# Gate logits as four column-strip products and a sum, rank offsets in a 97th row, a bank held for values and logits

## The chip, the cores and the metric

One core of one Trainium2 chip. The metric is the device time of one execution in microseconds (us). The engines are TensorE (PE in the profile, its weight loads PEld), VectorE (DVE), ScalarE (ACT), GpSimd (POOL) and the sync engine (SP), which issues most DMAs. Each engine works through its own queue in order.

## The reference

```python
q_d, k_d, v_d = means over groups of 4 positions of q, k, v        # B,H,S,D = 4,8,576,64
out = repeat(softmax(scale*q_d@k_d.T) @ v_d, 4) \
    + softmax(where(|i-j|<4, scale*q@k.T, -1e9)) @ v
x = out.transpose(0,2,1,3).reshape(2304, 512)
logits = x @ w_gate + modality_bias[modality_id]                   # 512 x 8
e_idx = argmax(logits); gate_w = softmax(logits)[e_idx]
for e in range(8): x[mask_e] = gate_w * (relu(x[mask_e] @ w1[e]) @ w2[e])
h = x @ w_in; out = (max(h,0) + alpha*min(h,0)) @ w_out
```

## The kernel before

The kernel is one program of three parts: attention with the gate (`attention`, L16 to L373), the expert stage (`moe`, L612) and a dense second layer (`moe2`, L748). Attention goes over 4 batches with 6 tiles of 96 tokens each, 24 tiles in all. Each tile passes through small steps, and the loop at L356 traces them shifted against one another: `local1a`, `local1b`, `local1c` (scores in a band, softmax, its transpose into block-diagonal form), `local2` (values), `gate2` (transposes and logits), `gate3` (rank and row store). In turn n the loop traces `local1c` of tile n+1, `local2` of tile n, `local1a` of n+2, `gate3` of n-2, `gate2` of n-1 and `local1b` of n+2. Between them `go` (L360) traces pieces of the next batch's pooled attention (`stageA` to `stageP`) and, by `filler(4)`, four steps of the early expert.

The early expert (`Early`, L582): once some tiles are counted (turns in `EARLY`, L374), 128 rows of the likeliest expert are loaded and pushed through both of its layers, 640 matmul instructions at L596 for 5 slots of 128 rows, as filler between attention's matmuls. What is left is traced behind attention (L837, L839), and the expert stage's engines branch after the last of it (L874).

The order on each engine isn't the traced one. The tile framework plans it: every traced instruction has a priority (its place, moved ahead by `tc.high_priority`: 300 to 400 for the tile steps by `AHEAD`, L332), and the planner runs a model of the engines' times and gives each engine, whenever it is free in the model, the ready instruction of the best priority. On the chip each engine then takes its queue strictly in that order. The framework also puts in every semaphore wait.

PSUM has 8 banks: `pa` and `pb` for the early expert, and six here (L27): `sl` scores, `pv` values, `xb` transposed rows, `lg` logits, two `tp`. The rank tile `rk` and the counts share the bank of `lg` (L28, L821); each new tile of a bank waits until the last one is released.

The steps around the change:

- `local2` (L276): 8 value products into a `pv` tile of 128 x 4 x 96 (L283), each in one half of the array's columns. VectorE adds the pooled part (L286) and so makes `xt`, the tile's rows transposed: 128 partitions by 4 chunks of 96 tokens.
- `gate2` (L289): 4 transposes of `xt` (L294), which ScalarE copies to the row buffer (L295). Then the logits, 12 products: for each of 3 groups of 32 tokens, 4 chunks of 128 features are summed into 32 partitions of `p` (L299), with 32 columns of `xt` stationary and the 8 columns of the gate weights `wgs` moving. VectorE adds the bias (L300), finds the maximum and its index (L302, L303) and makes the one-hot `oh` (L305).
- `gate3` (L314): the rank of each token within its expert, summed in one bank: `tri` by `oh` (tokens before it in the tile), `ones` by `running` (tokens of the tiles before), and a single row of `ones` by `eoff`, the experts' row offsets 2304*e (L318 to L320). GpSimd makes the next `running` (L323), a rotating buffer of 96 x 8 (L126). VectorE picks out the rank (L325), and GpSimd stores the rows by an indirect DMA (L328).

An f32 product is two instructions in the profile (and two weight loads); a bf16 one and a transpose are one.

```python
for j in range(3):                                     # L297
    for c in range(4):
        nc.tensor.matmul(p[32*j:32*j+32],lhsT=xt[:,c,32*j:32*j+32],rhs=wgs[:,c],start=c==0,stop=c==3,tile_position=(0,32*j))
```

Of the kernel before, what the change touches and what calls it, by code (L numbers as in the profile page):

```python
# [4 lines left out]
F32=mybir.dt.float32; F32R=mybir.dt.float32r; BF16=mybir.dt.bfloat16; I32=mybir.dt.int32; U32=mybir.dt.uint32  # L5
# [4 lines left out]
N=B*S; DM=H*D; E=8  # L10
TT=96; NT=S//TT
# [4 lines left out]
def attention(ctx, tc, q, k, v, mod, wg, bias, xs, running, ps, eps, zeros, filler):  # L16

    nc=tc.nc
    sm=ctx.enter_context(tc.tile_pool(name="a_small",bufs=6))
    xp=ctx.enter_context(tc.tile_pool(name="a_rows",bufs=1))  # L20
    cp=ctx.enter_context(tc.tile_pool(name="a_const",bufs=1))
    X=[xp.tile([TT,4,132],F32,name=f"x{i}") for i in range(4)]
    wk=ctx.enter_context(tc.tile_pool(name="a_work",bufs=2))
    loading=ExitStack(); ld=loading.enter_context(tc.tile_pool(name="a_load",bufs=1))

    FIRST=dict(sd00="pa",sd01="pb",sd02="pa",sd03="pb")
    BANKS=dict(sl=1,pv=1,xb=1,lg=1,tp=2)  # L27
    SAME=dict(tl="tp",et="tp",pd="tp",sd="tp",rk="lg")  # L28
    def psum(shape,name):
        if name in FIRST: return eps.tile(shape,F32,tag=FIRST[name],name=name)  # L30
        k=name[:2]; k=SAME.get(k,k)
        return ps.tile(shape,F32,tag=k,name=name,bufs=BANKS[k])

    loads={}
    NB=S//128; TL=S-128*NB
    def load(b,which):
        if b>=B: return
        if which=="qk":
            for pair in (0,4,1,2,3):
                for n in "qk": load(b,(n,pair))  # L40
        elif type(which) is tuple:
            n,pair=which; src=(q if n=="q" else k)[b]
            if pair<4:
                t=loads[b,n,pair]=ld.tile([128,2,4*D],F32,tag="ld"+n,name=f"ld{n}{b}{pair}",bufs=3)
                nc.sync.dma_start(t,src[2*pair:2*pair+2,:512].rearrange("h (p r) d -> p h (r d)",r=4))
            else:
                t=loads[b,n,pair]=ld.tile([2*GT,4,4*D],F32,tag="lt"+n,name=f"lt{n}{b}")
                for h2 in range(2): nc.sync.dma_start(t[GT*h2:GT*h2+GT],src[h2::2,512:].rearrange("a (p r) d -> p a (r d)",r=4))
        elif which<2:
            w=loads["v",b,which]=ld.tile([128,4,4*D],F32,tag="ldv",name=f"ldv{b}{which}",bufs=2)  # L50
            nc.sync.dma_start(w,v[b,4*which:4*which+4,:512].rearrange("h (p r) d -> p h (r d)",r=4))
        else:
            w=loads["v",b,2]=ld.tile([128,4*D],F32,tag="ldw",name=f"ldw{b}")
            for h in range(H):
                nc.sync.dma_start(w[16*h:16*h+16],v[b,h,512:].rearrange("(p r) d -> p (r d)",r=4))
    load(0,"qk")
    wgs=cp.tile([128,4,E],F32,name="wgs")
    nc.sync.dma_start(wgs,wg.rearrange("(c p) e -> p c e",p=128))
    NTT=B*NT
    modi=cp.tile([TT,NTT,2],I32,name="modi")  # L60
    nc.sync.dma_start(modi,mod.rearrange("(t u) w -> u t w",u=TT))
# [44 lines left out]
    def iota_f(shape,pattern,base,cm,name,dt=F32):  # L106
        t=cp.tile(shape,dt,name=name)
        nc.gpsimd.iota(t,pattern=pattern,base=base,channel_multiplier=cm,allow_small_or_imprecise_dtypes=True)
        return t
    io8=cp.tile([TT,E],U32,name="io8"); nc.gpsimd.iota(io8,pattern=[[1,E]],base=0,channel_multiplier=0)  # L110
    eoff=cp.tile([1,E],BF16,name="eoff")
    eofff=iota_f([1,E],[[N,E]],0,0,"eofff"); nc.vector.tensor_copy(eoff,eofff)
    ones=cp.tile([TT,TT],BF16,name="ones"); nc.gpsimd.memset(ones,1.0)
    tri=cp.tile([TT,TT],BF16,name="tri"); nc.gpsimd.memset(tri,1.0)
    nc.gpsimd.affine_select(out=tri,in_=tri,pattern=[[1,TT]],compare_op=ALU.is_gt,fill=0.0,base=0,channel_multiplier=-1)
    tok=iota_f([TT,B*NT],[[TT,B*NT]],0,1,"tok")
# [3 lines left out]
    def bias_rows():  # L120
# [2 lines left out]
        for o,m,k2 in ((bsel,m0,0),(bse1,m1,1)):  # L123
            nc.vector.tensor_tensor(out=o,in0=m[:,:,None].to_broadcast([TT,NTT,E]),in1=bb[:,k2:k2+1].to_broadcast([TT,NTT,E]),op=ALU.mult)
        nc.vector.tensor_tensor(out=bsel,in0=bsel,in1=bse1,op=ALU.add)
    def new_running(n): return cp.tile([TT,E],BF16,tag="running",name=f"running{n}",bufs=3)  # L126
    running[0]=new_running(-1); nc.vector.memset(running[0],0.0)

    qd={}
    def stageA(b,pair,n):  # L130
# [145 lines left out]
    def local2(b,t):  # L276

        bd=st.pop((b,t)); w=V.pop((b,t))
        p=psum([128,4,TT],f"pv{b}{t}")
        for pair in range(4):  # L280
            for h2 in range(2):
                h=2*pair+h2
                nc.tensor.matmul(p[64*h2:64*h2+64,pair],lhsT=w[:,h],rhs=bd[:,h],start=True,stop=True,tile_position=(0,64*h2))  # L283
        xt=wk.tile([128,4,TT],F32,tag="xt",name=f"xts{b}{t}",bufs=3)
        c=t*TT//4
        nc.vector.tensor_tensor(out=xt.rearrange("p c (g r) -> p c g r",r=4),in0=p.rearrange("p c (g r) -> p c g r",r=4),  # L286
            in1=OT[b][:,:,c:c+TT//4,None].to_broadcast([128,4,TT//4,4]),op=ALU.add)
        st[b,t]=xt
    def gate2(b,t):  # L289

        xt=st.pop((b,t)); n=b*NT+t
        x=X[n%len(X)]
        px=psum([TT,4,128],f"xb{b}{t}")
        for c in range(4): nc.tensor.transpose(px[:,c],xt[:,c],ident)  # L294
        nc.scalar.copy(x[:,:,:128].rearrange("p a (c j) -> p c a j",c=4),px.rearrange("p c (a j) -> p c a j",a=4))  # L295
        p=psum([TT,E],f"lg{b}{t}")
        for j in range(3):  # L297
            for c in range(4):
                nc.tensor.matmul(p[32*j:32*j+32],lhsT=xt[:,c,32*j:32*j+32],rhs=wgs[:,c],start=c==0,stop=c==3,tile_position=(0,32*j))  # L299
        l=sm.tile([TT,E],F32,tag="l",name=f"l{b}{t}"); nc.vector.tensor_tensor(out=l,in0=p,in1=bsel[:,n],op=ALU.add)  # L300
        m8=sm.tile([TT,E],F32,tag="m8",name=f"m8{b}{t}"); i8=sm.tile([TT,E],U32,tag="i8",name=f"i8{b}{t}")
        nc.vector.max(out=m8,in_=l)  # L302
        nc.vector.max_index(out=i8,in_max=m8,in_values=l)  # L303
        oh=sm.tile([TT,E],BF16,tag="oh",name=f"oh{b}{t}")
        nc.vector.tensor_tensor(out=oh,in0=io8,in1=i8[:,0:1].to_broadcast([TT,E]),op=ALU.is_equal)  # L305
        ng=sm.tile([TT,4],F32,tag="ng",name=f"ng{b}{t}")
        gated[0]=d=nc.gpsimd.tensor_scalar(out=ng[:,0:1],in0=m8[:,0:1],scalar1=-1.0,scalar2=None,op0=ALU.mult)
        ex=sm.tile([TT,E],F32,tag="ex",name=f"ex{b}{t}")
        nc.scalar.activation(out=ex,in_=l,func=AF.Exp,bias=ng[:,0:1],scale=1.0,accum_out=ng[:,1:2])
        with tc.issue_after(d.ins): nc.gpsimd.tensor_copy(x[:,0,129:130],tok[:,n:n+1])  # L310
        gated[0]=d=nc.gpsimd.tensor_scalar(out=ng[:,1:2],in0=ng[:,1:2],scalar1=1e-9,scalar2=None,op0=ALU.add)
        nc.vector.reciprocal(out=x[:,:,128],in_=ng[:,1:2].to_broadcast([TT,4]))
        st[b,t]=(x,ng,oh)
    def gate3(b,t):  # L314

        x,ng,oh=st.pop((b,t))
        p=psum([TT,E],f"rk{b}{t}")
        nc.tensor.matmul(p,lhsT=tri,rhs=oh,start=True,stop=False)  # L318
        nc.tensor.matmul(p,lhsT=ones,rhs=running[0],start=False,stop=False)
        nc.tensor.matmul(p,lhsT=ones[0:1],rhs=eoff,start=False,stop=True)  # L320
        old=running[0]
        running[0]=new_running(b*NT+t)
        running[1]=nc.gpsimd.tensor_tensor(out=running[0],in0=old,in1=oh,op=ALU.add)  # L323
        jk=sm.tile([TT,E],F32,tag="jk",name=f"jk{b}{t}")
        nc.vector.tensor_tensor_reduce(out=jk,in0=p,in1=oh,scale=1.0,scalar=0.0,op0=ALU.mult,op1=ALU.add,accum_out=ng[:,3:4])  # L325
        ri=sm.tile([TT,1],U32,tag="ri",name=f"ri{b}{t}")
        nc.gpsimd.tensor_copy(ri,ng[:,3:4])
        d=nc.gpsimd.indirect_dma_start(out=xs[:],out_offset=bass.IndirectOffsetOnAxis(ap=ri[:,0:1],axis=0),in_=x.rearrange("p a d -> p (a d)"),in_offset=None,bounds_check=E*N-1,oob_is_err=False)  # L328
        tc.declare_no_dep(d.ins,group="early rows",reason="rows of other ranks than those of the early slots")
# [26 lines left out]
    for n in range(len(seq)+2):  # L356
        b,t=seq[n] if n<len(seq) else (B,0)
        if t==0 and b+1<B: fill=down(b+1)
        left=[P*(NT-t)-1]
        def go():  # L360
            step(max(1,left[0])); left[0]-=1
            filler(4)
        at(local1c,n+1)
        at(local2,n); go()
        go()
        go()
        at(local1a,n+2); go()
        at(gate3,n-2)
        at(loadV,n+3)
        at(gate2,n-1); go()  # L370
        at(local1b,n+2); go()
        yield n
# [538 lines left out]
```

## Time and profile before

| | us |
|---|---|
| median of 3 runs | 880.15 (875.56 to 884.18) |
| the profiled execution, its time | 872.86 |
| the profiled execution, its span | 871.1 |
| TensorE busy in the span | 813.2 |
| VectorE, ScalarE, GpSimd busy | 529.4, 361.4, 262.4 |

The profile is of one execution. Times in rows are microseconds from the start of the span; a row of a timeline gives the start, the time until its end, the engine, the line of the kernel, the operation and its output and inputs with their shape (for PE the stationary shape, then the moving one), how many instructions it merges, and in brackets how long the engine was idle before and what ended that. PE's rows overlap, since a matmul starts while the one before it is still leaving the array: what a group takes of TensorE is the time from its start to the start of the next group.

### The profile page before, as it was taken

To read this page: it belongs to the slowest core of one execution; us is meant where nothing else is said; L and a number is where in the kernel's file an instruction comes from. 1 tells how busy PE (TensorE), PEld (TensorE's weight loads), DVE (VectorE), ACT (ScalarE), POOL (GpSimd) and SP (SyncE) were. 2 spreads that over 40 slices of the span, in tenths; PEclk is the share of its full clock that TensorE was granted. 3 is DMA by queue.
4 is the path that set the end of the run, shared out by engine and by line. 5 is a ranking of instruction groups with operands and counts; after the bars stand their busy time and mean duration, and the time that the engine had idled before them with its cause. 6 is when DMAs were issued, how large, how long until landed. Compare 5 with 4: busy or idle time off the path is not lost.

```text
span 871.1 us, 16800 instructions
## 1 busy us (share of the span) xinstructions
PE 813.2 (93%) x6175; PEld 696.5 (80%) x6175; DVE 529.4 (61%) x1304; ACT 361.4 (41%) x863; POOL 262.4 (30%) x450
## 2 busy tenths in 40 slices
PE   5788899989997989899899999999999999999997
PEld 3466677778897989899898888888888888888895
DVE  6865866666444998989747997443444333433361
ACT  7687796885423655656442333111121111111120
POOL 9424645366332556534322342100010001000100
PEclk9786899999999999999999999999999999999999
DMA  7635666322333524549402342200020001000000
GB/s 190 174 98 157 189 176 171 103 59 55 78 86 91 99 86 110 111 135 245 107 25 75 132 147 71 85 1 0 11 82 1 0 1 64 3 0 1 38 13 25
DMA packets 96610, 71.74 MB, mean 82 GB/s; under 512 B 40457, under 2 KB 83977, under 8 KB 96521
## 3 DMA queue, kind: packets, MB, share of 16 engines
q1 hardware_dynamic: 93544, 61.02, 26.7%
q0 software_dynamic: 2976, 9.59, 3.2%
q8 instruction: 50, 0.82, 0.4%
q14 instruction: 40, 0.32, 0.2%
HBM read 76.43 MB, written 18.90 MB: 109 GB/s over the span
## 4 chain that ended last, share of the span: by engine, by line
PE 51%; issue 1%; DVE 1%; DMA 0%; POOL 0%; ACT 0%; POOLq 0%; DVEq 0%
PE oh L777 23%; PE oy L768 22%; PE y L721 3%; PE h L701 3%; DMA out<-o,ti 0%; POOL L L573 0%; DVE xwo L550 0%; DVE hl L704 0%; POOLq L907 0%; DVE w1l L542 0%; DVE xwi L549 0%; ACT o L793 0%; DVE xl L542 0%; ACT wih L541 0%; ACT yo L724 0%
## 5 line engine op out<-in xcount | busy, mean ns | idle before, releaser
L541 ACT CAST gh<-m 128x512 fp32r<-128x512 f32 (+1 forms) x80 | 44.5, 556 | 241.3 <-DVE m L780 239.4
L777 PE MATMUL oh<-oxh,wil 128*128 128x512 f32 (+1 forms) x320 | 118.9, 372 | 0.0
L777 PE MATMUL oh<-oxh,wih 128*128 128x512 f32 (+1 forms) x320 | 118.9, 371 | 0.0
L777 PE MATMUL oh<-oxl,wih 128*128 128x512 f32 (+1 forms) x320 | 118.6, 371 | 0.0
L779 DVE TENSOR_SCALAR m<-oh,al 128x512 f32<-128x512 f32 (+1 forms) x80 | 55.5, 694 | 91.1 <-PE oh L777 91.1
L794 POOL DMA_INDIRECT out<-o,ti x18 | 17.6, 979 | 307.8 <-ACT o L793 270.4
L768 PE MATMUL oy<-woh,gh 128*128 128x512 f32 x272 | 107.1, 394 | 0.0
L768 PE MATMUL oy<-wol,gh 128*128 128x512 f32 x272 | 106.7, 392 | 0.0
L768 PE MATMUL oy<-woh,gl 128*128 128x512 f32 x272 | 106.5, 393 | 0.0
L701 PE MATMUL h<-xh,w1h 128*128 128x256 f32 x224 | 66.5, 297 | 12.4 <-DVE hl L704 6.8
L542 DVE TENSOR_TENSOR gl<-m,gh 128x512 fp32r<-128x512 f32 (+1 forms) x80 | 48.9, 611 | 40.1 <-ACT gh L541 40.0
L777 PEld LDWEIGHTS oh<-oxh,wil 128*128 128x128 f32 x320 | 60.2, 188 | 11.8
L777 PEld LDWEIGHTS oh<-oxh,wih 128*128 128x128 f32 x320 | 60.1, 188 | 11.5
L777 PEld LDWEIGHTS oh<-oxl,wih 128*128 128x128 f32 x320 | 60.1, 188 | 11.3
L701 PE MATMUL h<-xl,w1h 128*128 128x256 f32 x224 | 65.2, 291 | 0.0
L701 PE MATMUL h<-xh,w1l 128*128 128x256 f32 x224 | 64.8, 290 | 0.0
L721 PE MATMUL y<-hh,w2h 128*128 128x256 f32 x224 | 62.1, 286 | 2.6 <-DVE yo L723 2.0
L721 PE MATMUL y<-hh,w2l 128*128 128x256 f32 x224 | 61.2, 287 | 0.9 <-DVE w2l L542 0.9
L768 PEld LDWEIGHTS oy<-woh,gl 128*128 128x128 f32 x272 | 51.1, 188 | 12.1
L768 PEld LDWEIGHTS oy<-wol,gh 128*128 128x128 f32 x272 | 51.0, 188 | 11.4
L721 PE MATMUL y<-hl,w2h 128*128 128x256 f32 x224 | 59.6, 286 | 0.5 <-DVE hl L704 0.4
L768 PEld LDWEIGHTS oy<-woh,gh 128*128 128x128 f32 x272 | 51.1, 188 | 11.0
(303 smaller groups left out, 1868.4 us busy)
## 6 DMA issues: line engine op xcount, KB each, us to landing
wraw<-in_moe_w SPq DMA_DIRECT2D x56, 512.0 KB
wi<-in_moe_w_in SPq DMA_DIRECT2D x32, 256.0 KB
wo<-in_moe_w_out SPq DMA_DIRECT2D x32, 256.0 KB
vw<-in_v SPq DMA_DIRECT2D x88, 64.0 KB
xs<-z SPq DMA_DIRECT2D x8, 528.0 KB
ldq<-in_q SPq DMA_DIRECT2D x16, 256.0 KB
ldk<-in_k SPq DMA_DIRECT2D x16, 256.0 KB
ldv<-in_v SPq DMA_DIRECT2D x8, 512.0 KB
```

Of the source, the lines that this page charges most:

```text
L541: nc.scalar.copy(hi,x)
L542: return lo_engine.tensor_tensor(out=lo,in0=x,in1=hi.bitcast(F32),op=ALU.subtract)
L701: nc.tensor.matmul(h,lhsT=a[:,c],rhs=b[:,c],start=n==0,stop=n==11); n+=1
L721: nc.tensor.matmul(y,lhsT=a[:,f],rhs=b,start=n==0,stop=n==23); n+=1
L768: nc.tensor.matmul(y[t],lhsT=a[:,ts],rhs=b[:,f],start=f==0 and k==0,stop=f==15 and k==2)
L777: nc.tensor.matmul(h[:,:n],lhsT=a[:,c,fs],rhs=b[:,c,:n],start=k==0,stop=k==11); k+=1
L779: nc.vector.tensor_scalar(out=m[:,:n],in0=h[:,:n],scalar1=0.0,scalar2=al[:,f:f+1],op0=ALU.min,op1=ALU.mult)
L794: nc.gpsimd.indirect_dma_start(out=out[:],out_offset=bass.IndirectOffsetOnAxis(ap=ti[:,t:t+1],axis=0),in_=o[:],in_offset=None,bounds_check ...
```

## The change

The gate weights are padded from 8 to 32 columns with zeros (a fill on GpSimd ahead of their load). The logits of a tile become 4 products, one for each chunk of 128 features, with the padded weights stationary and the tile's 96 tokens moving; chunk c lands in partitions 32c to 32c+31, side by side. VectorE copies the 128 x 96 result to SBUF (`lq`), and one product with a constant matrix `sume` (1 where the partition's number modulo 32 is the expert's) sums the four chunks and turns the result back to tokens by experts.

The three `running` buffers get a 97th partition that holds the experts' offsets, written once; `ones` gets a 97th row, and the offsets' own product goes.

The `pv` bank is held by one tile, `PV`, for the whole of attention: 384 columns for the values, the rest for the partial logits and their sum. The logits no longer use the `lg` bank, which the rank and the counts keep.

```diff
-    BANKS=dict(sl=1,pv=1,xb=1,lg=1,tp=2)
+    BANKS=dict(sl=1,xb=1,lg=1,tp=2)
...
+    PV=ps.tile([128,512],F32,tag="pv",name="pv")
...
-    wgs=cp.tile([128,4,E],F32,name="wgs")
-    nc.sync.dma_start(wgs,wg.rearrange("(c p) e -> p c e",p=128))
+    wgs=cp.tile([128,4,32],F32,name="wgs"); nc.gpsimd.memset(wgs,0.0)
+    nc.sync.dma_start(wgs[:,:,:E],wg.rearrange("(c p) e -> p c e",p=128))
...
-    eoff=cp.tile([1,E],BF16,name="eoff")
-    eofff=iota_f([1,E],[[N,E]],0,0,"eofff"); nc.vector.tensor_copy(eoff,eofff)
-    ones=cp.tile([TT,TT],BF16,name="ones"); nc.gpsimd.memset(ones,1.0)
+    eofff=iota_f([TT+1,E],[[N,E]],0,0,"eofff")
+    ones=cp.tile([TT+1,TT],BF16,name="ones"); nc.gpsimd.memset(ones,1.0)
+
+    sume=iota_f([128,E],[[-1,E]],128,1,"sume"); sumi=cp.tile([128,E],I32,name="sumi")
+    nc.vector.tensor_copy(sumi,sume)
+    nc.vector.tensor_scalar(out=sumi,in0=sumi,scalar1=31,scalar2=None,op0=ALU.bitwise_and)
+    nc.vector.tensor_copy(sume,sumi)
+    nc.vector.tensor_scalar(out=sume,in0=sume,scalar1=0.0,scalar2=None,op0=ALU.is_equal)
...
-    def new_running(n): return cp.tile([TT,E],BF16,tag="running",name=f"running{n}",bufs=3)
-    running[0]=new_running(-1); nc.vector.memset(running[0],0.0)
+    RUN=[cp.tile([TT+1,E],BF16,name=f"run{i}") for i in range(3)]
+    for t in RUN: nc.vector.tensor_copy(t[TT:TT+1],eofff[TT:TT+1])
+    running[0]=RUN[2][:TT]; nc.vector.memset(running[0],0.0)
...
-        p=psum([128,4,TT],f"pv{b}{t}")
+        p=PV[:,:4*TT].rearrange("p (c i) -> p c i",c=4)
...
-        p=psum([TT,E],f"lg{b}{t}")
-        for j in range(3):
-            for c in range(4):
-                nc.tensor.matmul(p[32*j:32*j+32],lhsT=xt[:,c,32*j:32*j+32],rhs=wgs[:,c],start=c==0,stop=c==3,tile_position=(0,32*j))
+        pq=PV[:,4*TT:]
+        for c in range(4): nc.tensor.matmul(pq[32*c:32*c+32,:TT],lhsT=wgs[:,c],rhs=xt[:,c],start=True,stop=True,tile_position=(0,32*c))
+        lq=wk.tile([128,TT],F32,tag="lq",name=f"lq{b}{t}")
+        nc.vector.tensor_copy(lq,pq[:,:TT])
+        p=pq[:TT,TT:TT+E]
+        nc.tensor.matmul(p,lhsT=lq,rhs=sume,start=True,stop=True)
...
-        nc.tensor.matmul(p,lhsT=ones,rhs=running[0],start=False,stop=False)
-        nc.tensor.matmul(p,lhsT=ones[0:1],rhs=eoff,start=False,stop=True)
+        n=b*NT+t
+        nc.tensor.matmul(p,lhsT=ones,rhs=RUN[(n+2)%3],start=False,stop=True)
         old=running[0]
-        running[0]=new_running(b*NT+t)
+        running[0]=RUN[n%3][:TT]
```

## Rows read from the trace of the kernel before

**Rows 1.** The page, its first lines: span, busy time, share and instructions.

```profile
span 871.1 us, 16800 instructions
```

**Rows 2.** Stretches: length, then busy time of PE, PEld, DVE, ACT, POOL; granted clock.

```profile
0.00:80.00 80.00, 58.55 (x583) 42.11 (x583) 52.76 (x151) 63.09 (x142) 41.17 (x116) 0.83 0.60 158
80.00:200.00 120.00, 106.45 (x1476) 87.36 (x1480) 80.57 (x324) 94.27 (x251) 63.85 (x144) 0.93 0.50 136
200.00:254.00 54.00, 54.00 (x757) 48.10 (x749) 25.50 (x138) 22.61 (x76) 25.97 (x67) 1.00 0.26 67
254.00:277.00 23.00, 22.83 (x201) 22.41 (x200) 14.76 (x63) 6.76 (x22) 5.91 (x7) 1.00 0.44 112
```

**Rows 3.** Timeline of PE, 274 to 283 us: the expert stage's first matmul.

```profile
282.24 0.58 PE L701 MATMUL h<-xh,w1h 128*128 128x256 f32 x1 [5.41 <-ACT w1h L541]
```

**Rows 4.** PE's waits, 0 to 255 us: total, times, longest.

```profile
PE sl L252 <- ACT kb L150: 11.0, 7, 3.2
...
PE et L215 <- DVE ed L197: 1.0, 2, 0.5
```

**Rows 5.** Timeline of PE, 242 to 256 us: logits, rank and early matmuls.

```profile
247.05 0.72 PE L299 MATMUL lg<-wgs,xts 128*32 128x8 f32 x24
247.70 2.05 PE L596 MATMUL ph<-Te,wraw 128*128 128x128 f32 x16
249.59 0.17 PE L318 MATMUL rk<-oh,tri 96*96 96x8 bf16 x1
...
249.74 0.20 PE L320 MATMUL rk<-eoff,ones 1*96 1x8 bf16 x1
249.87 1.16 PE L596 MATMUL ph<-Te,wraw 128*128 128x128 f32 x8
```

**Rows 6.** Timeline of PE, 140 to 180 us: shapes near to the new ones.

```profile
140.13 0.72 PE L205 MATMUL sd2t<-kdb,qdb 128*32 128x144 f32 x16
140.78 0.94 PE L596 MATMUL py<-eh,wraw 128*128 128x128 f32 x6
...
171.64 0.88 PE L283 MATMUL pv<-bd,vw 128*64 128x96 f32 x16
172.45 0.64 PE L294 MATMUL xb<-ident,xts 128*96 128x128 f32 x4
172.93 0.17 PE L318 MATMUL rk<-oh,tri 96*96 96x8 bf16 x1
```

**Rows 7.** Timeline of PE, 165 to 200 us: values and transposes in turn.

```profile
180.04 0.38 PE L283 MATMUL pv<-bd,vw 128*64 128x96 f32 x2
...
180.60 0.38 PE L283 MATMUL pv<-bd,vw 128*64 128x96 f32 x2
```

**Rows 8.** DVE's groups, 40 to 255 us: total and mean ns, then idle before.

```profile
L286 DVE TENSOR_TENSOR xts<-pv,ot 128x384 f32<-128x384 f32 x24 | 13.0, 543 | 4.7 <-PE pv L283 4.4 <-PE lg L299 0.2
...
L300 DVE TENSOR_TENSOR l<-lg,bsel 96x8 f32<-96x8 f32 x24 | 3.7, 154 | 14.4 <-PE lg L299 12.1 <-PE py L596 2.2
```

**Rows 9.** Timeline of all engines, 86 to 101 us: from VectorE to TensorE.

```profile
89.94 0.08 DVE L325 DVE_READ_ACCUMULATOR2_ANT ng<- 96x1 f32 x1
...
90.07 0.72 PE L299 MATMUL lg<-wgs,xts 128*32 128x8 f32 x24 [0.26 <-DVE ng L325]
```

**Rows 10.** Timeline of all engines, 224 to 256 us: values around the logits.

```profile
227.12 0.55 PE L283 MATMUL pv<-bd,vw 128*64 128x96 f32 x8
...
227.60 0.73 PE L299 MATMUL lg<-wgs,xts 128*32 128x8 f32 x24
...
228.25 0.38 PE L283 MATMUL pv<-bd,vw 128*64 128x96 f32 x2
228.36 0.16 DVE L300 TENSOR_TENSOR l<-lg,bsel 96x8 f32<-96x8 f32 x1 [2.82 <-PE lg L299]
```

**Rows 11.** Timeline of all engines, 0 to 24 us: the identity and its reader.

```profile
2.30 0.19 POOL masks.py:197 MEMSET ident<- 128x128 f32 x1
...
4.05 1.12 PE L140 MATMUL tpq<-ident,ldq 128*128 128x128 f32 x4 [4.05 <-POOL ident masks.py:199]
```

## The prediction

> **What bounds the kernel now.** I read the stage table first, then TensorE's waits, then its order of instructions around one gate step, then VectorE's groups. The profiled execution has a span of 871.1 us inside a time of 872.86 us [rows 1], 1.8 us around it, and it lies 7.3 us under the median of the three runs shown, 880.15 us. All sums below are differences, taken on the profiled execution and set on the median.
>
> The reader is to see four stages in the table [rows 2]. From 0 to 80 us TensorE is busy 58.6 of 80 us, at a mean granted clock of 0.83. From 80 to 200 us it is busy 106.5 of 120. From 200 to 254 us it is busy all 54.0 of 54, at clock 1.00: the last attention tiles, with the early expert's matmuls as filler between them. From 254 to 277 us it works off the rest of those early matmuls, 22.8 of 23 us. After that nothing of TensorE runs until 282.24 us, where the expert stage begins behind ScalarE's weight split [rows 3]. That gap begins when the last early output has left, so the end of the early work moves everything behind it. The change touches attention only; everything after 282 us I take as shifted, not altered.
>
> So the question is what happens to TensorE's queue up to 277 us. Up to 255 us its largest wait is for ScalarE's copies of the keys, 11.0 us in 7 times; the largest total that it waits for VectorE at one place is 1.0 us [rows 4]. In the first 200 us a shorter TensorE queue is partly given back to ScalarE; after 200 us it is gained in full, because there TensorE waits for nobody.
>
> **Part 1: the logits.** Before, a tile's logits are 12 products, 24 instructions (each f32 product is two). They start at 247.05 and the next matmul starts at 247.70: 0.65 us, 27 ns each [rows 5]. After, there are 4 products, 8 instructions, each on its own 32 columns of the array with 96 moving columns, and then one sum product, 2 instructions with 96 stationary and 8 moving columns. No row shows these shapes, so I bound them. The partial products: nearest is a group of the same array width with 144 moving columns, 16 in 0.65 us (140.13 to 140.78), 8 of them 0.33; by columns that is 0.22. At the old spacing of 27 ns, 8 take 0.22. The values' products, two column strips instead of four and the same 96 moving columns, take 0.81 for 16 (171.64 to 172.45), 0.41 for 8 [rows 6]. I take 0.30, between, nearest to the same array width. The sum: a transpose with 96 stationary columns takes 0.12 (four from 172.45 to 172.93 [rows 6]), so two instructions 0.24; at the low end 2 x 27 ns = 0.05, at the high end the 0.24 and one change of the array's layout, 0.17 [rows 7] (worked out below), 0.41. I take 0.26, by the row of its own width. So 0.56 against 0.65, 0.09 saved, between 0.38 saved and 0.17 lost. Over 24 tiles 2.2 us, from 9.1 saved to 4.1 lost.
>
> **Part 2: the rank.** Three bf16 products become two. The third starts at 249.74 and the next matmul at 249.87 [rows 5]: 0.13 us each, 3.1 us over 24 tiles. That is the high end; the low end is a third of what all three take (249.59 to 249.87), 0.09 us, 2.2 us in all. A product less in the queue has nothing to lose. One more row in the contraction of the remaining product I take at nothing: its instructions and their columns stay as they are.
>
> Together TensorE's queue is 5.3 us shorter, 0.22 us a tile. Eight tiles have their logits after 200 us, and gain in full: 1.8 us. For the other 16 I take half, since in the stages where they lie TensorE has waits that ScalarE ends: 1.8 us of 3.5. That is 3.6 us gained.
>
> **Part 3: the new copy.** VectorE gets one copy from PSUM a tile, 128 partitions by 96. Between the 8-column add, 0.154 us, and the 384-column add, 0.543 us [rows 8], the line gives 1.03 ns a column, so 0.245 us; 24 of them 5.9 us. After 200 us VectorE is busy 25.5 of 54 us and hides it. Before, it is busy about two thirds (52.8 of 80, 80.6 of 120) [rows 2], and TensorE hardly waits for it; but ScalarE and GpSimd wait for it too, so I charge a tenth, 0.6 us; from 0 to all of it, 5.9 us.
>
> **Part 4: the new wait.** The sum product stands in TensorE's in-order queue and waits for that copy. Everything behind it waits along: the transposes, the scores of tiles ahead and the early expert's matmuls. A release costs little: the accumulator read before the logits ends at 90.02 and their weights start loading at about 90.07 [rows 9], 0.05 us. With VectorE free, the wait is 0.05 for the hop, 0.245 for the copy and 0.05 back, 0.35 us, and 0.17 to 0.25 more for the last partial product to leave the array: 0.5 us in all. It is hidden whenever five early instructions (16 take 1.89 us, 247.70 to 249.59 [rows 5], 0.12 each) or a tile's scores stand between. From about 100 us on there is such filler at nearly every step, and the planner puts ready work ahead of a waiting instruction, so I take nothing. Without that cover it is 0.5 us a tile, 12 us in all, and more where VectorE has a queue.
>
> **Part 5: the held bank.** Values and logits now share one bank, and I take it that the framework keeps writer and reader of one bank apart: a tile's value products cannot run while VectorE reads another's logits. Before they did mix: the values' products at 227.12 and 228.25 stand around the logits at 227.60, and VectorE reads the logits at 228.36 [rows 10]. The bank's turn is 0.81 values, 0.54 add, 0.30 partial, 0.25 copy, 0.26 sum, 0.15 add and six hops of 0.05: 2.6 us, in a tile that takes about 240/24 = 10 us. I take nothing for it; the low end is a gain, since the logits no longer alternate with the rank product in one bank (the one wait for that in TensorE's list up to 255 us is the 0.26 us of [rows 9]), the high end the 2.6 us at the four last tiles, about 10 us.
>
> **Part 6: the start.** A fill of the padded gate weights stands ahead of the identity on GpSimd. TensorE's first transpose waits for the identity, 4.05 us [rows 11]. The identity's own fill, the same 128 x 128, is 0.19 us, so 0.2 us, and it goes straight through, as ScalarE copies without a pause after that. The gate weights' load now waits for the fill on the sync queue; twelve loads of queries and keys stand before it there, so nothing (a late fill would hold the value loads behind it: I allow 1 us). Six more tiny VectorE instructions, 0.15 us each by the 8-column add [rows 8], fall where VectorE waits for ScalarE anyway: 0 to 1 us, I take 0.
>
> **The sum.** 3.6 gained less 0.6 and 0.2: 2.8 us, so 870 us for the profiled execution and 877 us for the median.
>
> One rule is weighed here. The trace shows what alternating between array layouts costs: where two value instructions (51 ns each by [rows 6]) and one transpose (0.12) take turns, a round from 180.04 to 180.60 is 0.56 us instead of 0.22 [rows 7], 0.17 us a change. The Trainium skill, TensorEngine Tiling (Array Packing), section Key Properties, says that changing the tiling mode drains the engine. By that rule, which these rows bear out, the sum product costs nothing extra between full-width early matmuls and two changes among the scores; that is one of the rivals.
>
> **The rivals.** First, slower: the sum product stands right behind the partial products, or behind a VectorE queue, in most tiles. For it: VectorE is over 60% busy up to 200 us, and its queue holds adds and reductions of 0.4 to 0.7 us. Against it: filler, and the planner knows of the wait. Price 0.5 to 1.0 us a tile, 12 to 24 us, less the 5.3 saved: 7 to 19 us slower, 890 us in the middle. It decides from 0.22 us a tile on; from 0.6 us on it shows beyond 1%.
>
> Second, the changes of layout: in the 16 tiles before 200 us the sum falls among scores and values, two changes of 0.17 us each: 5.4 us, which takes the gain away: 880 to 883 us, no change.
>
> Third, faster by more: the separate banks let the gate run earlier, the early slots start sooner, and their matmuls fill TensorE's idle time of 13.5 us between 80 and 200 us [rows 2]. With half of that, 6.8 us on top of 2.8: 871 us. Against it: TensorE's waits there are ScalarE's, and the logits rarely waited for the bank.
>
> Fourth, the planner makes another order of the whole stage from its own durations; single orders can lie 5 us to either side. This widens the range, without a sign.
>
> **How the numbers follow.** The forecast (within 4 us of 877) has 0.42, the layout changes 0.15, the stall 0.23, the faster gate 0.20. A measurement of this kernel tells about 1%, 8.8 us, from no change. The faster gate is over that in most cases, the forecast and the planner's order in a few: 0.26 faster. The stall is beyond it in about four of five: 0.19 slower. That leaves 0.55. The range goes from 866 (faster gate, and logits at their low bound) to 889 (stall at the low half of its price).
>
> **What would show it.** Right: the 8 partial instructions in 0.22 to 0.41 us; the rank group 0.13 us shorter; about 0.25 us for the copy; the end of the early matmuls near 274 us instead of 277. Wrong: TensorE waits for the copy as a new row of over 3 us in its list of waits; full-width sums between scores; value products waiting for the logits' add; an end of the early work at or after 277 us.

## The result, and the profile after

| | before | after |
|---|---|---|
| median of the runs beside each other, us | 878.22 | 890.0 (886.02 to 891.08) |
| ratio, 95% interval | | 1.0132 (1.0089 to 1.0174) |
| span of the profiled execution, us | 871.1 | 888.4 |
| maximum of the last tile's logits on VectorE starts, us | 251.92 | 272.74 |
| last count on TensorE starts, us | 254.87 | 274.64 |
| first matmul of the expert stage starts, us | 282.24 | 297.29 |

Slower by 1.3%, 1 us outside the range of 866 to 889 us. In a later job, beside another set of runs of before, the same kernel stood at 1.0197 (1.0164 to 1.0231). The profiled execution of before is one of its faster ones (872.86 us, median 878.22), that of after lies at its median, so the spans differ by 17.3 us and the medians by 11.8. Of the 17.3 us, 15.1 are there when the expert stage starts. The page's first line, to [rows 1]:

```profile
span 888.4 us, 16132 instructions
```

The stages after, to [rows 2] (columns as there; the two behind the granted clock are the busy share of the DMA engines and the GB/s that they moved), with the stretch behind the early work:

```profile
0.00:80.00 80.00, 52.80 (x515) 38.14 (x517) 56.03 (x164) 63.82 (x144) 41.50 (x118) 0.86 0.59 149
80.00:200.00 120.00, 103.21 (x1291) 85.05 (x1290) 80.92 (x318) 90.65 (x247) 57.16 (x129) 0.92 0.51 131
200.00:254.00 54.00, 54.00 (x666) 47.85 (x657) 28.97 (x127) 23.02 (x74) 26.62 (x61) 1.00 0.40 82
254.00:277.00 23.00, 18.61 (x195) 16.90 (x193) 7.97 (x54) 5.51 (x21) 6.87 (x23) 0.98 0.16 40
277.00:297.00 20.00, 0.00 (x0) 0.00 (x0) 8.72 (x36) 1.43 (x2) 2.93 (x2) 0.50 0.34 81
```

TensorE is busy 156.0 us of the first 200, instead of 165.0, and 228.6 us of the first 277, instead of 241.8. What is new is the last line: 20 us in which it does nothing. Its timeline after, to [rows 3, 5, 6]:

```profile
95.41 0.45 PE L227 MATMUL et<-ident,edt 128*128 128x128 f32 x1 [3.17 <-DVE m L312]
...
240.71 0.17 PE L328 MATMUL rk<-oh,tri 96*96 96x8 bf16 x1
...
240.78 1.14 PE L606 MATMUL ph<-Te,wraw 128*128 128x128 f32 x8
241.85 0.37 PE L305 MATMUL pv<-xts,wgs 128*32 128x96 f32 x8
242.15 0.64 PE L302 MATMUL xb<-ident,xts 128*96 128x128 f32 x4
242.63 2.62 PE L606 MATMUL py<-eh,wraw 128*128 128x128 f32 x22
245.09 0.26 PE L309 MATMUL pv<-sume,lq 128*96 128x8 f32 x2
245.20 2.70 PE L606 MATMUL py<-eh,wraw 128*128 128x128 f32 x22
247.83 0.55 PE L291 MATMUL pv<-bd,vw 128*64 128x96 f32 x8
248.31 0.21 PE L328 MATMUL rk<-oh,tri 96*96 96x8 bf16 x1
248.38 0.19 PE L330 MATMUL rk<-run,ones 97*96 97x8 bf16 x1
248.49 0.55 PE L291 MATMUL pv<-bd,vw 128*64 128x96 f32 x8
...
269.16 2.25 PE L606 MATMUL py<-eh,wraw 128*128 128x128 f32 x18
...
274.64 0.17 PE L419 MATMUL cnt<-run,r_one 96*1 96x8 bf16 x1 [1.01 <-POOL run L333]
297.29 0.58 PE L711 MATMUL h<-xh,w1h 128*128 128x256 f32 x1 [22.48 <-DVE xwi L560]
```

And the same places before; the first four lines are for the part on the order:

```profile
66.93 1.55 PE L283 MATMUL pv<-bd,vw 128*64 128x96 f32 x16
68.41 0.49 PE L299 MATMUL lg<-wgs,xts 128*32 128x8 f32 x6
68.83 1.09 PE L294 MATMUL xb<-ident,xts 128*96 128x128 f32 x4
69.85 0.84 PE L299 MATMUL lg<-wgs,xts 128*32 128x8 f32 x18
...
254.87 0.17 PE L409 MATMUL cnt<-running,r_one 96*1 96x8 bf16 x1
254.96 7.41 PE L596 MATMUL py<-eh,wraw 128*128 128x128 f32 x64
262.21 7.47 PE L596 MATMUL ph<-Te,wraw 128*128 128x128 f32 x64
269.52 7.31 PE L596 MATMUL py<-eh,wraw 128*128 128x128 f32 x64
```

This is the finding. A count is a small product that adds up the tokens of each expert; the last one stands behind the last tile, and the plan of the expert stage is made of it. Before, the last count (L409) starts at 254.87 us with 192 early matmul instructions (96 products) behind it, 21.9 us of TensorE. After, the count is TensorE's last instruction ahead of the expert stage, at 274.64 us, and every early matmul is ahead of it. The early matmuls themselves end 5.4 us earlier than before (at 271.41 instead of 276.83 us), and TensorE's queue with the count ends 2.0 us earlier (at 274.81). But the expert stage needs what follows from the count: the plan, the first rows' load, their turn (transposition) and their split. Before, that ran under the early matmuls, which covered it; after, nothing of TensorE covers it. Its steps after, on the other engines:

```profile
275.18 0.18 DVE L459 TENSOR_REDUCE r_nr<-r_t 1x8 f32<-1x64 f32 x1
...
282.79 2.68 SPq L576 DMA_DIRECT2D L<-xs  x4
...
288.21 1.91 POOL L583 TENSOR_TENSOR L<-L 128x1024 f32<-128x1024 f32 x1 [10.09 <-DMA L<-xs]
290.16 1.25 DVE L585 STREAM_TRANSPOSE T<-L 128x1024 f32<-128x1024 f32 x1 [7.67 <-POOL L L583]
291.48 1.04 ACT L551 CAST xh<-T 128x1024 fp32r<-128x1024 f32 x1 [16.74 <-issue]
...
296.62 1.66 ACT L551 CAST w1h<-wraw 128x512 fp32r<-128x512 f32 x3 [4.09 <-DVEq L887]
```

Plan 7.6 us (275.18 to 282.79), load 5.4, turn and first half of the split of the rows 4.3 (to 292.52), then the branch, at which ScalarE waits 4.1 us, and the first weights' split, until 297.29.

Why is the count so late? One part shows in the middle of the timeline after. A tile's partial products start at 241.85, its sum only at 245.09, the next tile's values at 247.83: in both gaps stand 22 early matmuls, 2.5 and 2.6 us. The values must not enter the held bank before VectorE has read the sum, so one tile's turn is over before the next one's begins. TensorE hardly stalls for it. The group of its sum, up to 276 us (total us and mean ns, then idle before):

```profile
L309 PE MATMUL pv<-sume,lq 128*96 128x8 f32 x48 | 7.3, 224 | 0.4 <-DVE lq L307 0.4
```

VectorE's copy, in its groups from 40 to 275 us:

```profile
L307 DVE COPY lq<-pv 128x96 f32<-128x96 f32 x24 | 6.0, 249 | 12.9 <-PE pv L305 12.8
```

The idle time in front of all 48 sum instructions is 0.4 us. The wait is filled, but with the very matmuls that covered the plan.

The larger part is older than these turns. The sixth and the sixteenth maximum of the logits, before:

```profile
100.25 0.17 DVE L302 MAX8 m<-l 96x8 f32<-96x8 f32 x1
...
199.82 0.17 DVE L302 MAX8 m<-l 96x8 f32<-96x8 f32 x1
```

And after:

```profile
111.39 0.15 DVE L312 MAX8 m<-l 96x8 f32<-96x8 f32 x1
...
215.14 0.17 DVE L312 MAX8 m<-l 96x8 f32<-96x8 f32 x1
```

The gates are 11.1 us late at the sixth of 24 tiles, 15.3 at the sixteenth and 20.8 at the last. The pause at 92 to 95 us (last section) lies just ahead of the sixth; what else delayed them before 215 us was not taken apart.

### The profile page after: what moved, and what is told of

It reads as the page before. It is cut to its first block, busy times and chain, and to the rows that moved or that the text cites. A ratio compares the mean times of both kernels' runs of the same rounds, so it can differ in the third digit from the quotient of the medians.

```text
span 888.4 us, 16132 instructions
## 1 busy us (share of the span) xinstructions
PE 800.9 (90%) x5815; PEld 686.1 (77%) x5815; DVE 546.3 (61%) x1334; ACT 361.0 (41%) x863; POOL 265.7 (30%) x452
## 4 chain that ended last, share of the span: by engine, by line
PE 52%; DVE 6%; DMA 4%; issue 3%; SPq 1%; POOLq 0%; ACT 0%; DVEq 0%; ACTq 0%
PE oh L787 23%; PE oy L778 22%; PE h L711 4%; PE y L731 3%; DMA wi<-in_moe_w_in 2%; DMA L<-xs 2%; DVE w2l L552 1%; DVE xwi L561 1%; DVE xwi L560 1%; DVE hl L714 1%; DVE xwi L559 1%; DVE w1l L552 1%; DMA wo<-in_moe_w_out 0%; DMA out<-o,ti 0%; DVE xl L552 0%
## 5 line engine op out<-in xcount | busy, mean ns | idle before, releaser
L711 PEld LDWEIGHTS h<-xh,w1h 128*128 128x128 f32 x224 | 45.4, 203 | 34.0 <-ACT w1h L551 23.3
L787 PEld LDWEIGHTS oh<-oxh,wil 128*128 128x128 f32 x320 | 60.2, 188 | 11.8
```

The source lines that it names most:

```text
L711: nc.tensor.matmul(h,lhsT=a[:,c],rhs=b[:,c],start=n==0,stop=n==11); n+=1
L787: nc.tensor.matmul(h[:,:n],lhsT=a[:,c,fs],rhs=b[:,c,:n],start=k==0,stop=k==11); k+=1
```

## The experiments

The products behind the last count are early products of the planned order (of 320 in all, two instructions each); the two times are starts in each kernel's trace, as above. The ratio is to runs of before in the same job.

| kernel | products behind the last count | last count, us | first expert matmul, us | ratio |
|---|---|---|---|---|
| before | 96 | 254.87 | 282.24 | 1 |
| after | 0 | 274.64 | 297.29 | 1.013, 1.020 |
| rank alone | 104 | 267.58 | 301.23 | 1.021 |
| bank alone | 80 | 262.37 | 289.62 | 1.012 |
| partials and sum alone | 0 | 289.11 | 310.43 | 1.038 |
| rank, partials and sum | 0 | 283.87 | 304.84 | 1.033 |
| rank and bank | 64 | 268.05 | 291.85 | 1.011 |
| after, 64 products held back | 64 | 265.54 | 291.64 | 1.012 |
| after, 88 held back | 88 | 267.40 | 296.33 | 1.014 |
| before, plan uncovered | 0 | 279.96 | 298.01 | 1.014 |
| before with one tiny copy | 83 | 277.94 | 305.10 | 1.028 |
| before with the setup alone | 80 | 260.72 | 287.85 | 1.002 |
| after, sum in the rank tiles' bank | 44 | 264.00 | 283.77 | 1.010 |
| after, another order | 0 | 274.32 | 296.55 | 1.017 |
| sum in the rank bank, order 2 | 100 | 259.58 | 289.42 | 1.011 |
| sum in the rank bank, order 3 | 83 | 261.04 | 288.72 | 1.003 |
| before, another order | 96 | 263.71 | 291.78 | 1.000 |

The times come from one profile each and rank the kernels only roughly: from the first expert matmul to the end of the span the profiles take 587 to 596 us. The setup alone starts the expert stage 5.6 us later than before and is no slower; the sum in the rank tiles' bank starts it 1.5 us later and is 1.0% slower.

**The price of the lost cover.** In the kernel before, the last count was queued behind the last early matmul, nothing else changed (the first cut of the edit, which keeps hold of that matmul as `early.last`, is left out):

```diff
...
-            with tc.high_priority(500): router.plan(psum,running,cp)
-        early.go(len(early.steps)-10)
-        mark=early.mark
-        early.finish()
+            early.go(len(early.steps)-10)
+            mark=early.mark
+            early.finish()
+            with tc.high_priority(500), tc.issue_after(early.last.ins): router.plan(psum,running,cp)
```

> The kernel before, nothing of the change in it; only the plan's count is queued behind the last early matmul on TensorE, so that all 320 early products stand ahead of it instead of 224. Cover theory: TensorE's work ends at about 277 us as before, the count with it, TensorE then idles 22 us as in the changed kernel instead of 5.4, the expert stage starts at 296 to 301 us and the time is 885 to 893 us beside some 876. If the plan were hidden anyway, or the loss lay in the logits' own chain, the time stays within 5 us of the kernel before.

1.0135 (1.0064 to 1.0206). Its timeline of TensorE:

```profile
279.96 0.17 PE L409 MATMUL cnt<-running,r_one 96*1 96x8 bf16 x1
298.01 0.58 PE L701 MATMUL h<-xh,w1h 128*128 128x256 f32 x1 [17.88 <-ACT w1h L541]
```

That is a loss of the changed kernel's size, 15.8 us at the start of the expert stage against 15.1 and nearly the same ratio, without any part of the change. (3.2 us of the 15.8 are early matmuls that end at 280.0 instead of 276.8, in a slightly other order.) So an uncovered plan is enough for a loss of this size.

**Giving cover back.** The changed kernel with early steps held until the last count is traced: 64 products (its edit is shown, cut), then 88.

```diff
     def go(self, n):
+        if self.hold: return
...
-        early.go(len(early.steps)-10)
+        early.hold=False
+        with tc.issue_after(router.marks[ENG.PE].ins):
+            early.go(len(early.steps)-10)
...
```

> The changed kernel, with the last early slot's matmuls held back until the last count has been issued on TensorE (traced behind attention and queued behind the count). If what costs the time is that the early matmuls ran ahead of the last gate steps and left the plan and the first row load uncovered, the count comes 10 us or more earlier than 274.6, some 15 us of early matmuls lie behind it, the expert stage starts 10 to 20 us before 297 us, and the time is 870 to 880 us. If the tiles are late by the length of their own chains, with or without filler between them, the count stays after 265 us and the time near 885 to 890, or above, since the held matmuls then come on top.

> The changed kernel with 88 of the 320 early products queued behind the last count, in place of none (the first trial held 64). Cover theory: the count comes at 258 to 264 us, early matmuls run until about 282, the expert stage starts some 5 us after them, 870 to 880 us. Rival: without filler in the last tiles TensorE idles there by as much as is won behind, and the time stays at 882 to 888 us as in the first trial.

64 held: 1.0123 (1.007 to 1.0176), the expert stage 5.7 us earlier than after; 88 held: 1.0142 (1.007 to 1.0213), 1.0 us earlier. Neither gained time that can be told from the changed kernel's, and both missed what the cover alone had promised, 870 to 880 us. With 64 held the count came at 265.54 us, 9.1 earlier than after but 10.7 later than before. With 88 it came no earlier, and the last early matmuls left at 291.1 us, 5.2 us before the expert stage: now the early work itself was late.

The trace with 64 held shows two reasons. Attention's own chain is late already where filler still stands: the twentieth maximum starts at 244.77 us, before at 228.56. And without filler the new waits lie open and the granted clock falls. Two rows of TensorE's timeline, and a stretch (columns as in [rows 2]):

```profile
251.78 0.34 PE L309 MATMUL pv<-sume,lq 128*96 128x8 f32 x2 [0.38 <-DVE lq L307]
252.38 0.88 PE L291 MATMUL pv<-bd,vw 128*64 128x96 f32 x16 [0.26 <-DVE l L310]
```

```profile
257.00:266.00 9.00, 4.10 (x32) 2.82 (x32) 3.31 (x23) 1.37 (x5) 4.20 (x14) 0.50 0.16 44
```

TensorE is busy 4.1 of 9 us at a granted clock of 0.50, and the first 64 early matmul instructions behind the count take 9.4 us (265.64 to 275.06), before 7.3 (254.96 to 262.21). So these two runs do not measure the cover alone.

**One part, or two.** The rank part alone, the bank alone, the partial products and sum alone (in the bank of `lg`), and two pairs; each is the corresponding lines of the diff.

> The kernel before with the rank part alone: three running buffers with a 97th row, one product less per tile. Bank theory and round-trip theory: the gate's last count stays near 255 us with some 20 us of early matmuls behind it, and the 24 x 0.13 us make the time 1 to 3 us shorter, 875 to 878 us beside 878. Order theory (any edit makes the planner lay the stage out anew): the last count can move by 5 us or more, and the time by as much, either way.

> The kernel before with the held bank alone: the 12 old logit products write behind the values in one tile that is held for all of attention. Bank theory: the value products of a tile wait for the logits' add of an earlier one, the last count moves from 255 us to 265 us or later behind the early matmuls, TensorE idles over 15 us before the expert stage, 885 to 892 us. Round-trip theory: no copy and no second product here, so 876 to 880 us with the last count near 255.

> The kernel before with the four partial products, the copy and the sum alone; they lie in the old bank of the logits, which they share with the rank, and the values rotate as before. Round-trip theory: the planner lays early matmuls between partial products and sum in each tile, the last count moves to 265 us or later, 885 to 892 us. Bank theory: the last count stays within 5 us of 255, 874 to 880 us.

> The changed kernel without the held bank: rank and the four partial products with their sum, these in the old bank shared with the rank. Round-trip theory: the count comes last on TensorE, with no early products behind it and 20 us or more of idle time, 887 to 906 us. Bank theory: the cover is back, 96 products or so lie behind the count, 872 to 880 us.

> The changed kernel without the partial products and their sum: rank and held bank with the 12 old logit products. Round-trip theory: some 60 to 100 early products lie behind the count, TensorE's idle time before the expert stage is 5 to 9 us, 876 to 886 us. Bank theory: the count comes late behind the early products, with 15 us or more of idle time, 886 to 895 us.

All were slower: 1.0212 (1.0162 to 1.0262), 1.0115 (1.0063 to 1.0166), 1.0378 (1.0327 to 1.043), 1.0326 (1.0255 to 1.0397) and 1.011 (1.0037 to 1.0183). Of these, the two with the sum have their count last, the three without it keep 64 to 104 products behind. The sum alone was slower than either theory had it (905.8 us against 885 to 892 at most), and the bank alone fell between them. But the rank alone, which takes a product away and adds only three small copies to the setup, lost 2.1%, more than the whole change. Its work doesn't explain that, and it led to the next two.

**The order by itself.** The kernel before with one copy of 8 numbers more in its setup; and with the setup of the change (the fill of the padded weights, the constant matrix, three copies into the 97th partition), its loop as before.

```diff
+    nul=cp.tile([1,E],BF16,name="nul"); nc.vector.tensor_copy(nul,eofff)
     running[0]=new_running(-1); nc.vector.memset(running[0],0.0)
```

> The kernel before with one copy of 1 x 8 elements more on VectorE in the setup, and nothing else: no work to speak of (0.2 to 1.5 us of VectorE near 20 us). But the planned order is another one: 237 early products instead of 224 stand ahead of the last count, and TensorE's queue has 88 changes of the array's layout ahead of the first count instead of 69. If the order is what costs (the rank alone had 95 such changes and lost 2%): slower by 0.5 to 2%, 882 to 893 us beside 877, the gates late by the end of the first batch. If only the work counts: no change, within 0.3%.

> The kernel before with the setup of the change and nothing of its loop: the fill of the padded weights, the constant matrix, the three copies into the 97th partition (the loop doesn't read them). If the start is what delays the gates (first maximum at 61.2 us instead of 55.5): slower by 2 to 6 us, with the first maximum at 59 to 62 us and that lag kept to the last count. If the start is absorbed, as the two traces suggest at the second and third tile: within 0.3%, unless the order differs again; planned are 240 early products ahead of the count and 51 layout changes ahead of the first count, fewer than before.

The one copy cost 25 us: 1.0283 (1.0241 to 1.0324), more than the 0.5 to 2% expected. The whole setup cost nothing that can be told: 1.0018 (0.9982 to 1.0055). So a planned order alone can be worth more than the change. One thing that the copy's order does, in its timeline of TensorE:

```profile
63.96 0.45 PE L295 MATMUL xb<-ident,xts 128*96 128x128 f32 x1
64.34 0.59 PE L284 MATMUL pv<-bd,vw 128*64 128x96 f32 x4
64.86 0.45 PE L295 MATMUL xb<-ident,xts 128*96 128x128 f32 x1
```

A stretch of it, in the table of stretches (columns as in [rows 2]):

```profile
64.00:72.00 8.00, 8.00 (x64) 4.86 (x63) 3.46 (x14) 4.08 (x8) 3.35 (x8) 0.50 0.42 110
```

And the same stretch before:

```profile
64.00:72.00 8.00, 6.49 (x60) 4.58 (x62) 4.00 (x13) 6.81 (x16) 1.35 (x2) 0.59 0.52 132
```

Transposes and values of two tiles take turns one by one, at a granted clock of 0.50: 3.90 us for 16 values and 4 transposes (63.96 to 67.86, where the next group starts). Before, at a like clock, they stand apart, 1.48 and 1.02 us. The Trainium skill, TensorEngine Tiling (Array Packing), section Key Properties, says that a change of the tiling mode drains the engine; the trace agrees so far as the turns cost time, 1.4 us more a tile at the low clock. The kernel with the rank alone shows the same turns between 62 and 76 us. How much of the 25 us they make was not taken apart.

**Is it order or structure?** The planner's priorities were moved by small amounts, and the orders it made were counted: in all 20 of the changed kernel the 320 early products are ahead of the last count, in 20 of before 224 to 268. These are planned orders, and no trace shows them, but one of the changed kernel was run:

```diff
-    AHEAD={local1a:300,local1b:400,local1c:300,loadV:350,local2:300,gate2:300,gate3:350}
+    AHEAD={local1a:300,local1b:415,local1c:300,loadV:365,local2:360,gate2:300,gate3:350}
...
-            with tc.high_priority(250): f[0](*f[1:])
+            with tc.high_priority(290): f[0](*f[1:])
```

> The changed kernel with other priorities of the planner (values 360 instead of 300, their loads 365, scores 415, pooled steps 290): the same instructions in another order, 219 changes of layout up to the last count instead of 234 (38 instead of 46 ahead of the first count), and still all 320 early products ahead of the last count. If the uncovered plan is the cause: still slower than before by 1 to 2%, the count last on TensorE, the expert stage's first matmul some 22 us behind the count. If the changed kernel only had an unlucky order: as fast as before, within 0.5%.

1.0169 (1.0124 to 1.0214), with the count last again and the same gap behind it:

```profile
274.32 0.17 PE L419 MATMUL cnt<-run,r_one 96*1 96x8 bf16 x1 [1.04 <-POOL run L333]
296.55 0.58 PE L711 MATMUL h<-xh,w1h 128*128 128x256 f32 x1 [22.06 <-DVE xwi L560]
```

So that the count comes last belongs to the change and not to one order. How much the change costs is less sure: its 1.3 to 2.0% lie within what the orders of the kernel before cost by themselves, from nothing to 2.8%.

**The turn of the held bank.** The sum product goes to the rank tiles' bank, so that the held bank is free when the copy has read it. The changed kernel ran beside it.

```diff
-        p=pq[:TT,TT:TT+E]
+        p=psum([TT,E],f"lg{b}{t}")
```

> The changed kernel with the sum product put into the bank of the rank tiles, so that the held bank is free for the next values once the copy has read it. If the turns of the held bank (values, add, partials, copy, sum, bias add, each a hop) set the gate's pace: the last maximum comes 4 to 12 us earlier than 272.7, the last count at 262 to 270 with 44 early products behind it as planned, and the time is 881 to 886 us. If the sum and the rank tiles get into each other's way in that bank, as without the held bank: 895 us or more.

> The changed kernel as it is, on the chip of this job, to stand beside the one with the sum in the other bank: 1.013 of the kernel before, its last count behind all early matmuls, the expert stage 15 us later than before.

880.95 us against 889.48 of the changed kernel: 1.0095 (1.0064 to 1.0127) against 1.0197 (1.0164 to 1.0231). The last maximum starts at 261.25 us, 10.1 us earlier than in the changed kernel beside it (271.31). Its timeline of TensorE:

```profile
256.83 0.37 PE L305 MATMUL pv<-xts,wgs 128*32 128x96 f32 x8
257.14 0.34 PE L309 MATMUL lg<-sume,lq 128*96 128x8 f32 x2
...
264.00 0.17 PE L419 MATMUL cnt<-run,r_one 96*1 96x8 bf16 x1
...
283.77 0.58 PE L711 MATMUL h<-xh,w1h 128*128 128x256 f32 x1 [9.58 <-ACT w1h L551]
```

The sum at 257.14 is that of the tile before the partials at 256.83: two tiles overlap, as the held bank forbids, and 44 products are left behind the count. In the two other orders below it is 100 and 83, in both orders of the changed kernel that were run none. The turn of the bank, held from the partials to the reading of the sum, is what took the cover. The sum alone and the rank with the sum have no held bank, but partials and sum in one tile of the rank tiles' bank; there the count comes last too. What the turn does not explain is the start: the sixth maximum is at 111.15 us here, and 109.76 in the changed kernel beside it.

**A better order for it.** The sum in the rank tiles' bank with the priorities of the run above (order 2), and in a third order; and the kernel before in another one (330 and 392 for two score steps).

> The same priorities, with the sum product in the rank tiles' bank: 220 early products ahead of the last count, so 100 behind it (23 us), and 237 changes of layout (48 ahead of the first count). By the cover the last count comes at 252 to 260, the expert stage starts 5 us behind the last early matmul, near 280, and the time is 0.99 to 1.00 of before. If the sum's longer way slows the gates whatever the order: 1.005 or more, with the last count after 262.

> The sum in the rank tiles' bank in a second order (values 315, their loads 342, pooled steps 290, three early steps instead of four at a time): 237 early products ahead of the last count, 83 behind it (19 us), 219 changes of layout (48 ahead of the first count). By cover and changes together: 0.985 to 1.00 of before. If orders differ by what neither count shows: anywhere within 2.5%.

> The kernel before with two priorities moved (330 and 392 for the scores instead of 300 and 400): the same instructions, 224 early products ahead of the last count as before, 221 changes of layout instead of 251, 58 instead of 69 ahead of the first count. If the changes of layout are what an order costs, 30 fewer at 0.17 to 0.3 us give 5 to 9 us: 0.99 of before. If the order of before was a lucky one in other ways: 1.005 to 1.02.

1.0106 (1.006 to 1.0151), 1.0031 (1.0002 to 1.006) and 0.9997 (0.9958 to 1.0036); 1.00 or less was hoped for in the first two, and 0.99 in the last. With the same priorities the sum in the other bank is again faster than the changed kernel (884.41 us against 891.19), and with a third order the loss is almost gone. But with the cover whole the end of the early work comes later (order 2: 284.3 us, 5.1 before the expert stage): late gates make the early counts late, and the early slots start behind those (the count ahead of the last one at 223.69 us, before 216.66; the slot's first matmul at 267.81, before 262.21). No version of the sum beat the kernel before. And 30 layout changes fewer in before brought nothing that can be told, where 5 to 9 us were expected of them: their number is no measure of an order. Whether those that stand at the low clock on the gates' chain are one was not taken apart.

## Why the prediction was wrong

- **The parts' own costs.** The partial products take 0.30 us (241.85 to 242.15), as taken. The sum takes 0.11 (245.09 to 245.20), where I took 0.26 by the row of its width: the low end was nearer. The two rank products take 0.07 (240.71 to 240.78) to 0.18 (248.31 to 248.49), 0.10 to 0.21 less than three, where 0.13 was my high end. So TensorE saves 0.34 to 0.45 us a tile, 8 to 11 us in all, where I took 5.3. The copy is 249 ns, against 245. The start cost nothing that lasted, as the setup alone shows, though the "tiny" instructions were mis-sized (below).
- **The end of the queue, near the forecast by luck.** TensorE's queue ended 2.0 us earlier, against 2.8, but by other terms. It was busy 13.2 us less up to 277 us, and idle 11.2 us more up to its end (35.0 to 46.2). The rows of its list of waits up to 277 us that VectorE ends sum to 15.5 us, before to 3.7; part 3 charged 0.6 for a busier VectorE. The early matmuls alone ended at 271.41 us, earlier than the 274 that was to show the forecast right, and the kernel was slower.
- **The step that failed** stands in the first part: "the end of the early work moves everything behind it". It was true of the kernel before, by 5.4 us, and I took it for a law. After, the early work ended 5.4 us earlier and the expert stage started 15.1 us later. Two chains meet there: the early work, with 5.1 to 5.4 us behind it where it alone is late (before, 88 held back, order 2), and the count, with 18 to 23 us behind it (18.1 in the uncovered kernel, 22.6 after). Before, the second ended first because 21.9 us of matmuls lay behind the count. I never looked up where the count stood. The two are not all: with the bank alone, rank and bank, the setup alone and 64 held, the stage starts 8.3 to 9.2 us behind the last early matmul and 23.8 to 27.3 behind the count, so that something else came last. In the setup alone SyncE issues the store of the last early rows 2.6 us behind ScalarE's last copy of them, after three loads of weights; the others were not followed up.
- **Part 4, "so I take nothing".** The wait is hidden, as I said: 0.4 us in all. Where the filler is held back it shows: 0.38 us for the copy and 0.26 for the bias add. What hides it was not free. It was the cover of the plan.
- **Part 5, "I take nothing for it".** The sum's place in the held bank is worth 8.5 us (880.95 against 889.48), and 6.8 with the other priorities (884.41 against 891.19), each time with the order that comes with it: toward the high end of 10 us. I priced the bank's turn by its instructions and hops, 2.6 us, and left out what the planner puts between them: 5.1 us of early matmuls in the turn shown.
- **The rivals.** The stall at the sum product gave 890 us, the number measured, by a mechanism that didn't happen: TensorE waits 0.4 us there, not 12 to 24. (Its own terms, 7 to 19 us above 880, have their middle at 893, so the match is luck twice.) The fourth, another order, had the size wrong: 5 us to either side, where one copy moved 25 us. Because of it, what the single parts cost can't be read from one order each; the sizes of the rank alone and the bank alone stay open, and so does how much of the change's loss is the order that came with it.

## What to carry to other kernels

Filler (ready work that fills an engine's waits) is not free when it also covers something later: before adding a wait that filler hides, find out what that filler hides now, and how long the chain is that it covers. Where a planner orders the instructions, one run of an edit measures the edit and an order together: run a neutral edit too, and several orders of the same edit. A buffer that is held over a whole turn must be priced with everything that may stand between the turn's steps, not by the steps alone.

## What the runs showed of the hardware

A tiny copy on VectorE took up to 3 us. The three into the 97th partition:

```profile
19.79 4.54 DVE L134 CAST run<-eofff 1x8 bf16<-1x8 f32 x3
```

One took 0.16 us, one 1.57 and one 2.98, where I took 0.15 each, while GpSimd fills buffers and adds in SBUF, from 15.57 to past 24 us. The Trainium skill, SBUF — State Buffer, section Who interferes with whom, says that the two engines share one pair of ports under an exclusive lock. The rows fit it; no run here kept GpSimd still to show that this is the cause.

TensorE's granted clock fell after the engine had paused, here as in the kernel with 64 held. After the 3.17 us pause that ends at 95.41 us (it waited for VectorE, which had the gate's bias add, steps of the early plan and the pooled scores in one queue), the stretch after reads:

```profile
95.40:102.40 7.00, 6.99 (x67) 6.29 (x67) 4.65 (x23) 3.15 (x11) 3.14 (x8) 0.53 0.95 277
```

0.53 is nearly the lower of its two levels, 1.2 GHz, and in that stretch a pair of pooled value products takes 0.24 us (99.52 to 99.76) where before it took 0.12 at full clock (94.70 to 94.82). So the pause cost twice, once itself and once in what followed it; the gates are 3.4 us late at the fifth maximum, 95.19 us, and 11.1 at the sixth.
